# Three unread loads from GpSimd beside SyncE's stream, in a fused attention and gated-MLP decode kernel

## The chip, the core and the metric

The kernel runs on one core of one Trainium2 chip. The metric is the device time of one execution in microseconds. Before the change it is 127.67 us, the median of three runs (127.45 to 127.72).

## What is computed

One token of width 576 is normalised, and three terms are added: the token itself, an attention over the last 4,096 positions of a cache with 16 key/value heads (32 query heads), and a gated MLP.

```python
xn = _layernorm(x)
q = (xn @ wq)                               # 32 heads of 128
k, v = last W = 4096 rows of the caches     # 16 heads, each used by two query heads
p = softmax(q k^T * Dh ** -0.5)
A = (p v) @ wo
z = gelu(xn @ w_in)                         # 4608 wide
z1, z2 = z[:2304], layernorm(z[2304:])
B = (z1 * (w_sp * z2 + b_sp)) @ w_out
out = x + A + B
```

All inputs are bfloat16. The caches' last 4,096 positions are 16.8 MB each, the four weights together 17.4 MB, so some 51 MB pass from HBM into the core's buffers for one row of output.

## The kernel before

**Loads.** Nearly all bytes are loaded by SyncE, with each load covering all 128 partitions, in an order written out by hand (L104 to L119): wq in two pieces, then the caches in four batches of four heads each, mixed as k0, k1, v0, k2, v1, k3, then win, v2, v3, wo in two pieces and wout in four. One batch of k or v is 4 MB, 32 KB for each partition. ScalarE issues five tiny loads (x_row in three pieces, two scalars).

**Buffers.** The loaded tiles share two pools of two buffers each under one tag "u". A tile of SMALL width has 16,384 elements a partition: k0 to k3, v2 and wout. A tile of LARGE width has 20,736: wq, v0, v1, win, v3 and wo, in this order, so that wq, v1 and v3 use one buffer in turn and v0, win and wo the other. A batch of k or v fills only the first 16,384 elements (NU * DH). In v0, v1 and v3 the last 4,352 elements of each partition stay unused. A load into a buffer waits until the readers of the tile before it are done, and it waits for the writes of the tile before it.

**Work.** `turn(b)` transposes a batch of keys on VectorE (L209, eight pieces). `scores(b)` multiplies them with the query on TensorE (L254), takes the maximum and the exponential. `values(b)` multiplies the probabilities with a batch of v (L288) and reads only the first NU * DH elements of a tile. `z_all` and `gate` do the MLP's first half from win (L311). The order is turn and scores of batch 0 and 1, values 0, turn and scores 2, values 1, turn and scores 3, z_all and gate, values 2 and 3.

**End.** `row_of` (L376) adds up the output row in two banks: x_row, 32 row blocks of wo, 18 row blocks of wout. VectorE and ScalarE copy the two halves out (L388, L389), and SyncE and ScalarE store them.

**GpSimd** makes constants at the start: an identity, two cleared tiles (xw, zq) and two copies of the identity (L145, L147). The page counts 3.9 us of work for it, and its last instruction, the copy to perm, starts at 4.14 us. It issues no loads.

The scheduler is set to manual: each engine runs its instructions in the order of the program, and the waits between engines follow from the tiles that are read and written.

Of the kernel before, what the change touches and what calls it, by code (L numbers as in the profile page):

```python
# [18 lines left out]
DH = 128  # L19
# [6 lines left out]
NU = W // NJ  # L26
# [16 lines left out]
def kernel(  # L43
# [14 lines left out]
    nc = tc.nc  # L58
# [42 lines left out]
    kn, vn = {}, {}  # L101
# [43 lines left out]
    nc.gpsimd.tensor_copy(rep4[:], ident[:].rearrange("p (g q) -> p g q", g=4).unsqueeze(2).to_broadcast([P, 4, 4, 32]))  # L145
    perm = const.tile([P, 32, 4], BF16, name="perm")
    nc.gpsimd.tensor_copy(perm[:], ident[:].rearrange("p (q h) -> p h q", q=4))  # L147


    twice = const.tile([64, P], BF16, name="twice")  # L150
# [270 lines left out]
```

## Time and profile before

| | |
|---|---|
| median of three runs | 127.67 us |
| profiled execution | 127.53 us |
| its span | 125.7 us |
| mean granted TensorE clock | 0.81 |
| TensorE busy | 78.6 us (62% of the span) |
| VectorE busy | 64.3 us (51%) |
| ScalarE busy | 10.2 us (8%) |
| GpSimd busy | 3.9 us (3%) |
| data moved | 51.03 MB in 2,467 packets, mean 406 GB/s |

The page gives the busy time of each engine, the DMA queues with their packets, bytes and share of the time of all 16 DMA engines, the chain of work that ended last, and the groups of instructions with what they waited for. Busy shares are means over the whole span, and the stages differ, so stretches of the span are asked for one by one. "SPq" is SyncE's issuing of loads, which is not counted as busy time. Queue q1 carries SyncE's transfers, q10 those of ScalarE, q8 and q14 instructions.

### The profile page before, as it was taken

To read this page: it belongs to the slowest core of one execution; us is meant where nothing else is said; L and a number is where in the kernel's file an instruction comes from. 1 tells how busy PE (TensorE), PEld (TensorE's weight loads), DVE (VectorE), ACT (ScalarE), POOL (GpSimd) and SP (SyncE) were. 2 spreads that over 40 slices of the span, in tenths; PEclk is the share of its full clock that TensorE was granted. 3 is DMA by queue.
4 is the path that set the end of the run, shared out by engine and by line. 5 is a ranking of instruction groups with operands and counts; after the bars stand their busy time and mean duration, and the time that the engine had idled before them with its cause. 6 is when DMAs were issued, how large, how long until landed. Compare 5 with 4: busy or idle time off the path is not lost.

```text
span 125.7 us, 1318 instructions
## 1 busy us (share of the span) xinstructions
PE 78.6 (62%) x534; PEld 37.6 (30%) x534; DVE 64.3 (51%) x129; ACT 10.2 (8%) x19; POOL 3.9 (3%) x10
## 2 busy tenths in 40 slices
PE   0042750099823998297599646699375097969861
PEld 0032220034211333145234223234063044435540
DVE  6315233499839995330999451999444830010001
ACT  2101000000030000301000031000120011010001
POOL 8400000000000000000000000000000000000000
PEclk9999998559996589755559999689976855595899
DMA  4999899998999989899898999999899999999950
GB/s 102 515 420 438 382 480 438 396 490 365 480 427 394 480 365 490 386 448 469 375 480 386 497 422 422 414 397 480 386 459 443 386 432 442 393 430 411 411 207 0
DMA packets 2467, 51.03 MB, mean 406 GB/s; under 512 B 284, under 2 KB 414, under 8 KB 670
## 3 DMA queue, kind: packets, MB, share of 16 engines
q1 hardware_dynamic: 2450, 50.96, 95.0%
q8 instruction: 4, 0.07, 0.2%
q14 instruction: 1, 0.01, 0.0%
q10 hardware_dynamic: 12, 0.00, 0.0%
HBM read 50.96 MB, written 0.00 MB: 405 GB/s over the span
## 4 chain that ended last, share of the span: by engine, by line
PE 43%; DMA 37%; DVE 10%; ACT 5%; SPq 2%; issue 1%; ACTq 0%
PE s L254 30%; DMA wout<-in_B_w_out_dram 19%; DMA k<-in_A_k_cache_dram 18%; PE pv L288 4%; ACT p L274 4%; DVE kt L209 4%; PE z L311 3%; PE op L296 2%; DVE sm L257 2%; PE tr L265 2%; SPq L92 2%; PE fin L376 1%; PE su L278 1%; DVE pt L276 1%; DVE m L267 1%
## 5 line engine op out<-in xcount | busy, mean ns | idle before, releaser
L254 PE MATMUL s<-kt,zq 128*128 128x512 bf16 x128 | 37.2, 456 | 11.1 <-DVE kt L209 11.1
L209 DVE STREAM_TRANSPOSE kt<-k 128x1024 f32<-128x1024 f32 x32 | 36.4, 1205 | 3.9 <-DMA k<-in_A_k_cache_dram 3.9
L254 PEld LDWEIGHTS <-zq 128*128 128x128 bf16 x128 | 14.4, 112 | 32.8 <-issue 22.1
L288 PE MATMUL pv<-v,pt 128*32 128x512 bf16 x128 | 12.4, 557 | 0.0
L274 ACT ACTIVATE p<-sm,nm 128x1024 bf16<-128x1024 f32 x4 | 4.6, 1147 | 67.9 <-DVE nm L270 67.9
L299 DVE TENSOR_TENSOR o_t<-op,rm 128x8 bf16<-128x8 f32 x4 | 0.7, 166 | 17.2 <-PE op L296 17.2
L276 DVE STREAM_TRANSPOSE pt<-p 128x1024 bf16<-128x1024 bf16 x4 | 5.0, 1245 | 5.4 <-ACT p L274 5.4
L296 PE MATMUL op<-selu,pvs 128*128 128x8 f32 x32 | 5.9, 311 | 2.9 <-ACT pvs L293 2.9
L257 DVE CUSTOM_DVE_ANT_1 sm<-s,cm 128x512 f32<-128x512 f32 x8 | 5.4, 671 | 3.7 <-PE s L254 3.7
L296 PEld LDWEIGHTS op<-selu,pvs 128*128 128x128 f32 x32 | 5.5, 259 | 5.8 <-ACT pvs L293 5.8
L278 PE MATMUL su<-sel,l 128*128 128x8 f32 x8 | 1.8, 293 | 7.6 <-ACT p L274 7.6
L218 PE MATMUL q_ps<-wq,xw 128*32 128x512 bf16 x36 | 4.2, 626 | 3.0 <-DVE xw L187 2.4
L376 PE MATMUL fin<-wo,o_p 128*1 128x288 bf16 x64 | 5.8, 357 | 0.1
L156 PE MATMUL x_ps<-one_bf,x_row 1*64 1x1 bf16 x9 | 1.2, 248 | 7.4 <-DMA x_row<-in_A_x_dram 7.4
L288 PEld LDWEIGHTS <-pt 128*32 128x32 bf16 x128 | 4.0, 128 | 5.6 <-issue 4.8
L388 DVE CAST res<-fin 1x288 bf16<-1x288 f32 x1 | 0.4, 446 | 9.9 <-PE fin L376 9.9
L265 PE MATMUL tr<-ident_f,m 128*128 128x128 f32 x8 | 1.9, 326 | 3.9 <-DVE m L263 3.9
L376 PEld LDWEIGHTS <-o_p 128*1 128x1 bf16 x64 | 3.4, 103 | 2.3 <-DVE o_p L370 0.3
L278 PEld LDWEIGHTS su<-sel,l 128*128 128x128 f32 x8 | 1.4, 218 | 8.4 <-ACT p L274 8.4
L311 PE MATMUL z<-win,xw 128*32 128x288 bf16 x72 | 3.8, 392 | 0.0
L376 PE MATMUL fin<-wout,hv 128*1 128x288 bf16 x36 | 2.6, 285 | 1.5 <-DMA wout<-in_B_w_out_dram 1.5
L293 ACT COPY pvs<-pv 128x512 f32<-128x512 f32 x4 | 2.3, 585 | 14.3 <-PE pv L288 14.3
(88 smaller groups left out, 39.0 us busy)
## 6 DMA issues: line engine op xcount, KB each, us to landing
k<-in_A_k_cache_dram SPq DMA_DIRECT2D x4, 4096.0 KB
v<-in_A_v_cache_dram SPq DMA_DIRECT2D x4, 4096.0 KB, 39.0
win<-in_B_w_in_dram SPq DMA_DIRECT2D x1, 5184.0 KB
wq<-in_A_wq_dram SPq DMA_DIRECT2D x1, 3584.0 KB
wo<-in_A_wo_dram SPq DMA_DIRECT2D x1, 2880.0 KB
wo<-in_A_wo_dram SPq DMA_DIRECT2D x1, 1728.0 KB, 20.0
wout<-in_B_w_out_dram SPq DMA_DIRECT2D x1, 1296.0 KB
wq<-in_A_wq_dram SPq DMA_DIRECT2D x1, 1024.0 KB, 4.9
```

Of the source, the lines that this page charges most:

```text
L209: nc.vector.transpose(t[:].rearrange("p c n e -> p (c n e)").bitcast(FP32), kn[b][:, UK * DH * k:UK * DH * (k + 1)].bitcast(FP32).rearrang ...
L218: nc.tensor.matmul(q_ps[32 * g:32 * g + 32, :], lhsT=xw[:, r, :], rhs=wq_t[:, 2048 * r + 512 * g:2048 * r + 512 * (g + 1)], start=r == 0, ...
L254: nc.tensor.matmul(s_ps[:], lhsT=zq[:, b, ce, ZPAD - 8 * k4:ZPAD - 8 * k4 + P], rhs=kt[b, 4 * kk + k4][:, c, :, e], start=k4 == 0 and ce = ...
L257: nc.vector.tensor_tensor_reduce(out=sm[:, kk, :].rearrange("p (n s) -> p n s", s=HB), in0=s_ps[:].rearrange("p (n s) -> p n s", s=HB), in ...
L265: nc.tensor.matmul(tr[:], lhsT=m1[:].to_broadcast([P, P]), rhs=ident_f[:], start=True, stop=True)
L274: nc.scalar.activation(p[:], sm[:].rearrange("p k n -> p (k n)"), ACT.Exp, bias=nm[:], accum_out=l[:])
L276: nc.vector.transpose(p_t[b][:].rearrange("p k u m -> p (k u m)"), p[:])
L278: nc.tensor.matmul(su[:], lhsT=l[:].to_broadcast([P, P]), rhs=sel8[:], start=True, stop=True)
L288: nc.tensor.matmul(pv[32 * g:32 * g + 32, :].rearrange("p (n d) -> p n d", n=4), lhsT=p_t[b][:, kk, u, :], rhs=v4[:, kk, u, :, :], start=k ...
L296: nc.tensor.matmul(op[:], lhsT=pvs[:, DH * u:DH * (u + 1)], rhs=selu[:, 8 * u:8 * u + 8], start=u == 0, stop=u == 3)
L311: nc.tensor.matmul(zp[i][32 * g:32 * g + 32, :], lhsT=xw[:, r, :], rhs=win_t[:, FH * r + a:FH * r + a + HW], start=r == 0, stop=r == NR - ...
L376: nc.tensor.matmul(fin[g][32 * g:32 * g + 1, :], lhsT=col, rhs=w[:, HW * g:HW * (g + 1)], start=start, stop=stop, tile_position=(0, 32 * g))
```

## The change

Behind the copy to perm, GpSimd issues three loads. Each one takes eight rows (partitions 64, 68, ... 92) and, for each row, two parts from w_out that lie 1,024 rows of it apart. The parts have 32, 2,112 and 1,984 elements: 64, 4,224 and 3,968 bytes. The first and the second load go into the unused end of v0, the third into that of v1. Nothing reads what they bring.

```diff
     perm = const.tile([P, 32, 4], BF16, name="perm")
     nc.gpsimd.tensor_copy(perm[:], ident[:].rearrange("p (q h) -> p h q", q=4))
+
+
+    few = B_w_out[0:2048, :].rearrange("(m i r) n -> i m (r n)", m=2, i=8)
+    for b, a, n in ((0, 0, 32), (0, 64, 2112), (1, 0, 1984)):
+        nc.gpsimd.dma_start(
+            vn[b][64:96:4, NU * DH + a:NU * DH + a + 2 * n].rearrange("i (m c) -> i m c", m=2), few[:, :, a:a + n])
```

In the program that is built, TensorE, VectorE and ScalarE have the same instructions in the same order as before. GpSimd has three DMA issues more. The first waits for the same semaphore count that v0's cache load reaches on completion, the third for that of v1's. On SyncE, the load of win waits for the first two new loads in addition, and the load of v3 for the third.

## The prediction

> **What bounds the kernel now.** I first read the page's slices and DMA queues, because the change adds nothing but transfers.
>
> ```profile
> DMA  4999899998999989899898999999899999999950
> ...
> q1 hardware_dynamic: 2450, 50.96, 95.0%
> q8 instruction: 4, 0.07, 0.2%
> ...
> q10 hardware_dynamic: 12, 0.00, 0.0%
> ```
>
> The DMA row is 8 or 9 tenths in every slice from the second to the 38th. Queue q1 holds SyncE's loads: 50.96 MB in 95.0% of 16 engines' span, which is 0.95 x 16 x 125.7 = 1,910.6 engine-us, so one DMA engine moves 26.7 B/ns and sixteen 427 GB/s. The busy time by stretches (columns: length, PE, PEld, DVE, ACT and POOL busy, granted clock, DMA share, GB/s) shows where the stream starts and stops:
>
> ```profile
> 4.00:120.00 116.00, 76.23 (x504) 36.30 (x506) 60.89 (x124) 8.53 (x17) 0.53 (x2) 0.79 1.00 430
> 118.00:120.00 2.00, 1.36 (x24) 0.84 (x22) 0.00 (x0) 0.00 (x0) 0.00 (x0) 1.00 0.99 396
> 120.00:122.00 2.00, 1.16 (x21) 0.72 (x18) 0.00 (x0) 0.00 (x0) 0.00 (x0) 1.00 0.56 212
> 122.00:124.00 2.00, 1.17 (x18) 0.62 (x14) 0.45 (x1) 0.39 (x1) 0.00 (x0) 1.00 0.04 15
> ```
>
> From 4 to 120 us the engines are at share 1.00, with no gap to fill. At the end they do not stop together: 0.56, then 0.04. The last bytes come from a few engines that run late.
>
> Next I asked whether SyncE ever issues too late, since its loads wait for free buffers. Its timeline:
>
> ```profile
> 33.66 0.54 SPq L98 DMA_DIRECT2D v<-in_A_v_cache_dram  x1
> 47.78 0.54 SPq L98 DMA_DIRECT2D k<-in_A_k_cache_dram  x1
> 57.38 0.34 SPq L92 DMA_DIRECT2D win<-in_B_w_in_dram  x1
> 69.17 7.79 SPq L98 DMA_DIRECT2D v<-in_A_v_cache_dram  x2
> 96.15 0.81 SPq L92 DMA_DIRECT2D wo<-in_A_wo_dram  x2
> ```
>
> When wo is issued at 96.15 us, everything except wo (4.72 MB) and wout (2.65 MB) has been issued: 43.59 MB. Up to 96.1 us the profile counts 423 GB/s, so 40.65 MB have moved, and 2.9 MB, or 6.9 us of stream, are still queued. The same sum gives 16 us of queue when v3 is issued (76.4 us) and 14 us at win (57.38 us). So the queue never runs dry. The long PE and DVE rows of the chain of waits (L254, L209) are how a buffer comes free, and they have at least 6.9 us of slack. The end of that chain is the part that holds:
>
> ```profile
> 97.48 24.29 DMA wout<-in_B_w_out_dram
> 121.78 0.04 issue
> 121.82 1.39 PE fin L376 x18
> 123.21 0.43 DVE res L388
> ```
>
> The last 18 matmuls start as a piece of wout lands. The kernel ends when the slowest DMA engine has emptied its queue, plus a fixed tail of about 4 us.
>
> **The change, part by part.** It removes nothing. PE, DVE and ACT keep their instructions and their order; GpSimd gets three DMA issues after perm (L147), its last work, and SyncE gets two more semaphores to wait for.
>
> *When the loads run.* The first writes tile v0 and so waits, in the built program, for the completion of v0's cache load, which was issued ahead of it; the third waits the same way for v1's. The page gives 39.0 us to landing for v, and v0 was issued at 5.63: 44.6 us. v1 comes 8.39 MB later, at 430 GB/s 19.5 us: 64.1 us. Nothing stands behind these waits on GpSimd, so the waits cost nothing.
>
> *The new waits on SyncE.* win must wait for the first two loads, v3 for the third. win is issued at 57.38, 12.8 us after 44.6; v3 at 76.4, 12.3 us after 64.1. The nearest row for a load behind a full queue is a piece of wo at 20.0 us to landing, but that is time in its own queue. These loads come on a queue of their own, like q10's. Five small loads of q10 stand in the packet records one after another between 4.7 and 11.2 us, about 1.07 us each, that is behind one 28 KB packet of q1 each time. At a turn of 1.2 us per 32 KB packet, two or three turns are under 4 us. Taken at nothing. If the cover of 12 us were gone, win would still have 14 us and v3 16 us of queue ahead of them. What would be late next is the issue of wo, with 6.9 us. [...]
>
> *The bytes.* 16 x (64 + 4,224 + 3,968) = 132,096 B. Nothing hides them, since the engines have no idle time between 4 and 120 us: every byte pushes back what is queued behind it. Evenly over 16 engines it is 8,256 B each, at 26.7 B/ns 0.31 us.
>
> *The packets.* The packet records show 9 ns for a completion mark and 20 to 22 ns for a packet of 384 B. Four to six such small pieces per engine make about 0.05 us.
>
> *Bounds of the sum.* Below: zero, if only engines that do not end last get the bytes. Above: the slower foreign packets of the trace are q8's. Four packets of 16 KB took 0.2% of 16 x 125.7 = 4.0 us, 1.0 us each, or 16 B/ns. By that, 8,256 B take 0.50 us. If the same eight engines got all three loads, it would be 16,512 B, 0.62 us at q1's rate and 1.0 us at q8's. I take q1's rate, evenly, because these loads go from the same memory into the same buffers as q1's, while q8 carries instructions: 0.31 + 0.05 = 0.36 us.
>
> [...]
>
> *The sum.* The profiled execution took 127.53 us, 1.8 us more than its span of 125.7, and lies 0.14 under the median of 127.67. 127.53 + 0.36 = 127.89; on the median, 128.03 us. The three runs spread over 0.27 us, so 0.2% (0.26 us) is about what a measurement of this kernel can tell from no change. The forecast is just past it.
>
> **The rivals.**
>
> *The late engines are spared (not slower).* The end is set by few engines, as the 0.56 and 0.04 show; most stop earlier. If all three loads fall on the same eight engines and the late ones are among the other eight, the extra 0.67 us passes in their slack, and the time stays 127.67 (at a share of 0.56, 0.44 x 2 us = 0.9 us of the mean engine is idle between 120 and 122 us). It decides as soon as no late engine gets a row. For it: few late engines. Against: it needs both one fixed set of eight and the late ones outside it. Chance 0.12.
>
> *All on the late ones.* The same fixed set, with a late engine in it: 0.62 + 0.05, 128.34 us. [...] Chance 0.10.
>
> *A foreign packet is dear.* Changing queues costs as q8's packets do, 0.50 us plus 0.05, or more where the packet of q1 behind it restarts slowly: up to 0.8 us, 128.2 to 128.5 us. For it: q8's 16 B/ns. Against: q10's small loads ran beside the stream with the share at 1.00. Chance 0.13.
>
> *Each load has a fixed price on the stream.* The first piece of wq, 1 MB, landed after 4.9 us, and its bytes are 2.5 us at 427 GB/s, so 2.4 us were not bytes. Three times that is 7.3 us: 135 us. Against: it is latency of an empty queue. The five small loads of q10 fell into full stretches and left no hole. The same holds for a fixed price at launch, of which the profile has no row: with 0.5 to 1.5 us the time would be 128.5 to 129.5. Chance 0.04 together. [...]
>
> *Faster.* The late engines are late for something other than their own bytes, and q8's four packets of 1.0 us are the candidates. If the shifted stream made these fetches fall on engines when they have time to spare, up to that 0.9 us could come back at the end, 126.8 us. Nothing in the change moves PE's instructions, so I see no reason for it. Chance 0.11.
>
> **How the numbers follow.** The forecast, 0.36 us evenly on all engines, has 0.50; its own range with the spread of the runs is 127.85 to 128.25. Predicted: 128.03 us. For 8 in 10 the range leaves out the far part of the faster case and the fixed prices and takes in the spared and the dear ones: 127.55 to 128.5. Slower by over 0.2% (above 127.93) is most of the forecast (0.41 of its 0.50), the two dearer cases and the fixed price, 0.27: 0.68. Within 0.2% are the spared case's 0.12 and 0.08 of the forecast: 0.20. Faster is the last case's 0.11 and 0.01 of the forecast: 0.12.
>
> **What would show it.** Right: a third kind of packets, 48 of data and 0.13 MB, on a new queue at about 45 and 65 us; the share still 1.00 from 4 to 120; SyncE's issue of win, v3 and wo within 0.2 us of before; and the last wait of PE on wout ending about 0.36 us later than 121.78, with the same tail. Wrong: win or v3 issued later, a hole in the DMA share near 45 or 65 us, a last landing that has not moved, or a longer stretch around an unchanged span.

## The result and the profile after

The changed kernel takes 128.37 us, the median of four runs (128.29 to 128.49), against 127.65 us for the kernel before in four runs of the same measurement. The medians differ by 0.72 us. The ratio is 1.0062, with a 95% interval of 1.0050 to 1.0075, which makes 0.79 us, at least 0.6 and at most 1.0. The forecast was 128.03, so the direction and the wide range (127.55 to 128.5) held, but the measured loss is twice the forecast one and lies outside the forecast's own range of 127.85 to 128.25.

The profiled execution took 128.39 us with a span of 126.6 us. The 1.8 us around the span are as before, so the loss is inside. First the page's DMA queues (packets, MB, share of 16 engines):

```profile
q1 hardware_dynamic: 2450, 50.96, 94.6%
q0 software_dynamic: 112, 0.13, 0.3%
q8 instruction: 4, 0.07, 0.2%
```

The three loads are there on a queue of their own, q0. The line of q1 holds the surprise. The same 2,450 packets and the same bytes now take 0.946 x 16 x 126.6 = 1,916 engine-us, 5 more than the 1,911 of before (one digit of the share is worth 2). The packet records of the trace, added up, say 1,910.9 before and 1,915.4 after. SyncE's own packets have become slower, beyond being pushed back by the new ones.

The timelines of GpSimd and SyncE, from the loads on:

```profile
44.74 1.25 POOL L152 DMA_DIRECT2D v<-in_B_w_out_dram  x2 [40.20 <-DMA v<-in_A_v_cache_dram]
64.85 0.56 POOL L152 DMA_DIRECT2D v<-in_B_w_out_dram  x1 [18.86 <-issue]
```

```profile
57.27 0.33 SPq L92 DMA_DIRECT2D win<-in_B_w_in_dram  x1
69.06 7.80 SPq L98 DMA_DIRECT2D v<-in_A_v_cache_dram  x2
96.07 0.81 SPq L92 DMA_DIRECT2D wo<-in_A_wo_dram  x2
```

The loads are issued when the caches' batches v0 and v1 have landed (their last marks, in the table below, are at 44.02 and 63.80 us). win, v3 and wo are issued within 0.2 us of before, so the new waits delay nothing. The end, as stretches (the last two columns are DMA share and GB/s) and as the end of the chain:

```profile
4.00:120.00 116.00, 75.94 (x498) 36.16 (x499) 60.91 (x124) 8.53 (x17) 2.34 (x5) 0.79 1.00 429
118.00:120.00 2.00, 0.98 (x16) 0.57 (x13) 0.00 (x0) 0.00 (x0) 0.00 (x0) 1.00 0.99 399
120.00:122.00 2.00, 1.27 (x18) 0.78 (x18) 0.00 (x0) 0.00 (x0) 0.00 (x0) 1.00 0.79 306
122.00:124.00 2.00, 1.36 (x18) 0.78 (x17) 0.00 (x0) 0.00 (x0) 0.00 (x0) 1.00 0.14 50
```

```profile
97.40 25.16 DMA wout<-in_B_w_out_dram
122.61 1.41 PE fin L382 x18
124.01 0.43 DVE res L394
```

The share is 1.00 throughout as before, and the piece of wout that the last 18 matmuls wait for lands at 122.56 us in place of 121.78. Behind it the tail is the same. All of the loss is in the stream.

Where in the stream? In the packet records each of SyncE's 17 loads leaves sixteen completion marks (4-byte packets; with one for the store of the output, 273 on q1). I read them as one from each of the 16 DMA engines. The earliest, middle and last of the 16 marks, in us:

| mark | before | after |
|---|---|---|
| v0 | 42.28 / 42.56 / 44.22 | 42.25 / 42.52 / 44.02 |
| k2 | 52.01 / 52.28 / 53.93 | 51.99 / 52.36 / 54.09 |
| v1 | 61.73 / 61.99 / 63.65 | 61.72 / 62.13 / 63.80 |
| k3 | 71.44 / 71.70 / 73.36 | 72.16 / 72.43 / 74.03 |
| v3 | 103.15 / 103.47 / 105.06 | 103.87 / 104.17 / 105.80 |

The second load (packets at 51 to 53 us) delays some engines and not the earliest. Behind the third (packets at 68.8 to 70.6 us) all sixteen marks are 0.62 to 0.76 us late, the earliest too, though the load has eight packets of data and so at most eight engines carry its data. Part of that is bytes: in experiment 1 below, where hardly a packet becomes slow, the earliest mark of k3 is still at 71.90 us. In the packet records of before, the 32 KB packets that start between 68 and 72 us all took their usual 1.22 us. Here 31 of them between 68.3 and 71.2 us took 0.04 to 0.38 us longer. Around the second load none of them took over 1.25 us. The third load does something to SyncE's packets that the second, of nearly the same size, does not.

### The profile page after: what moved, and what is told of

Same layout as the page of the kernel before. It is cut to its first block, busy times and chain, and to the rows that moved or that the text cites. A ratio compares the mean times of both kernels' runs of the same rounds, so it can differ in the third digit from the quotient of the medians.

```text
span 126.6 us, 1325 instructions
## 1 busy us (share of the span) xinstructions
PE 78.6 (62%) x534; PEld 37.7 (30%) x534; DVE 64.3 (51%) x129; ACT 10.2 (8%) x19; POOL 5.7 (5%) x13
## 3 DMA queue, kind: packets, MB, share of 16 engines
q1 hardware_dynamic: 2450, 50.96, 94.6%
## 4 chain that ended last, share of the span: by engine, by line
PE 43%; DMA 37%; DVE 10%; ACT 5%; SPq 2%; issue 1%; ACTq 0%
PE s L260 29%; DMA wout<-in_B_w_out_dram 20%; DMA k<-in_A_k_cache_dram 17%; PE pv L294 4%; ACT p L280 4%; DVE kt L215 4%; PE z L317 3%; PE op L302 2%; DVE sm L263 2%; PE tr L271 2%; SPq L92 2%; PE fin L382 1%; PE su L284 1%; DVE pt L282 1%; DVE m L273 1%
## 5 line engine op out<-in xcount | busy, mean ns | idle before, releaser
L394 DVE CAST res<-fin 1x288 bf16<-1x288 f32 x1 | 0.4, 446 | 10.8 <-PE fin L382 10.8
L152 POOL DMA_DIRECT2D v<-in_B_w_out_dram x3 | 1.8, 603 | 59.1 <-DMA v<-in_A_v_cache_dram 40.2
```

## The experiments

**Theory A** blames the rows. In the records a cache load of 128 rows is 128 packets of 32 KB at 1.22 us each, and the marks of successive ones are 9.7 us apart, which is eight packets to an engine. The theory supposes that the loads of eight rows run on one half of the engines and on the other in turn, and that the third one's half is not the one that brings rows 64 to 92 in the loads of 128 rows. **Theory B** is the rival from the prediction: a GpSimd load is dear by itself, for its kind or its packets. Each experiment was timed against the kernel before on the same chip, and its excess is the ratio times that kernel's median. Where a few runs pull this number, the difference of the medians stands beside it. The code cuts show new lines against the changed kernel; lines that stay, and from experiment 2 on those that are replaced, are left out. The packet records do not name the DMA engine, so none of them shows which engines carry a load or bring a row. The runs show which rows are cheap for which load.

**1. The third load to rows 0 to 28.**

```diff
-    for b, a, n in ((0, 0, 32), (0, 64, 2112), (1, 0, 1984)):
+    for b, a, n, p in ((0, 0, 32, 64), (0, 64, 2112, 64), (1, 0, 1984, 0)):
         nc.gpsimd.dma_start(
-            vn[b][64:96:4, NU * DH + a:NU * DH + a + 2 * n].rearrange("i (m c) -> i m c", m=2), few[:, :, a:a + n])
+            vn[b][p:p + 32:4, NU * DH + a:NU * DH + a + 2 * n].rearrange("i (m c) -> i m c", m=2), few[:, :, a:a + n])
```

> Edit: the third load goes to rows 0, 4, ... 28 of v1's unused end, no longer to rows 64 to 92. Measured so far: the changed kernel is 0.72 us slower, of which the bytes explain 0.36; from the first landing of k3 (72.65 against 71.90 us) on, all sixteen DMA engines are 0.75 us late, also those that do not carry the third load. Theory A (rows): the three loads take the DMA engines in two halves in turn, and the third one runs on the half that does not serve rows 64 to 92 in the 128-row loads; its bytes are paid twice, by the engines that carry them and by those that serve the rows. With rows 0 to 28 they are paid once: +0.36 us over the kernel before, near 128.0, and GB/s in the stretch 68 to 72 us no longer falls. Theory B (the third load is dear by itself, for its 7,936-byte packets or for its moment): the rows do not matter, +0.72 us, near 128.4.

Measured: 128.10 us, ratio 1.0033 (1.0021 to 1.0045), +0.42 us. Nothing differs but the partitions that the third load writes. The page's line of q1, with a span of 126.4 us, is back at 1,911 engine-us, and near the third load two 32 KB packets take over 1.25 us, against some thirty in the change:

```profile
q1 hardware_dynamic: 2450, 50.96, 94.5%
q0 software_dynamic: 112, 0.13, 0.3%
```

The expected sign in GB/s was a poor choice. The stretch 68 to 72 us reads 506 before, 368 after and 424 here, but the engines run nearly in step with 32 KB packets (before, fourteen of the sixteen marks of k3 lie within 0.55 us), and a short stretch catches a packet more or less: before, the stretches of 2 us between 4 and 118 us read 307 to 601 GB/s. The marks and the packets' time are the measure. The third load is not dear by itself, and B falls.

**2. The second load to rows 0 to 28.**

```diff
+    for b, a, n, p in ((0, 0, 32, 64), (0, 64, 2112, 0), (1, 0, 1984, 64)):
```

The rest is as in experiment 1.

> Edit: the second load goes to rows 0, 4, ... 28 of v0's unused end; the third stays at rows 64 to 92. Theory A: now both large loads run on the half that does not serve their rows, and both are paid twice: +0.72 and another 0.3, about +1.0 us, near 128.7, with a second fall of GB/s near 52 us. Theory B: the second load is as cheap as in the changed kernel: +0.72 us, near 128.4.

Measured: 128.93 us, ratio 1.0107 (1.0085 to 1.0128), +1.37 us, which one run of 129.84 pulls up (by the medians +1.22). The same second load, cheap in the changed kernel, is now dear: the earliest mark of v1 is at 62.02 us and the middle one at 62.63 (61.72 and 62.13 in the changed kernel). In the packet records q1's packets take 1,925.5 engine-us, 14.6 more than before, and 32 KB packets of over 1.25 us stand around both loads, 20 at the second and 24 at the third. The loss is somewhat larger than A's 1.0.

**3. Without the third load.**

```diff
+    for b, a, n in ((0, 0, 32), (0, 64, 2112)):
```

> Edit: the third load is left out; the first and the second stay. Both theories: the second load delays only the eight engines that carry it, by 8,448 B at 26.7 B/ns = 0.32 us. If an engine that ends last is among them, +0.35 us, near 128.0; if all of them are in the other half, no change, near 127.65. It prices the second load alone, and by the difference to the changed kernel the third.

Measured: 128.01 us, ratio 1.0019 (1.0003 to 1.0034), +0.24 us. The earliest mark of k3 stays at 71.48 us (71.44 before), so not every engine is late, and still the end moves, if only just clear of noise. That fits a late engine among those that carry the bytes: the last mark of k3 goes from 73.36 to 73.99 us.

**4. Without the first load.**

```diff
+    for b, a, n in ((0, 64, 2112), (1, 0, 1984)):
```

> Edit: the first load (64-byte parts) is left out. If the loads take the two halves of the DMA engines in turn, the second load now runs on the half that the third had. Theory A: the second load is then the one on the half that does not serve its rows and is paid twice, the third once: again about +0.7 us, near 128.35, but the loss is seen near 52 us (the landing of k2 and v1 late on all engines) and not near 70 us. Theory B: the third load stays dear near 70 us, +0.7 us. If there is no turn (the same eight engines for each load), leaving out 1 KB changes nothing, neither the time nor the place.

Measured: 128.59 us, ratio 1.0063 (1.0050 to 1.0076), +0.80 us. The place was not where I expected it, for a reason of its own: without the small load ahead of it the 4,224-byte load waits for nothing and is issued at 4.48 us. (In the change the small load is the first on its queue too, and it does wait for v0. Why the two differ is not shown.) Its packets lie between 8.2 and 10.8 us, and all engines are late from there on (the second piece of wq has its earliest mark at 13.81 us against 13.22). The 32 KB packets between 68 and 72 us are of their usual length. That fits A, but place and turn changed together, so it was done again.

**5. The first load twice.**

```diff
+    for b, a, n in ((0, 0, 32), (0, 0, 32), (0, 64, 2112), (1, 0, 1984)):
```

> Edit: the first load (64-byte parts) is issued twice, the second copy behind the first one's completion; the other two loads as in the changed kernel. It asks whether the loads take the two halves of the DMA engines in turn. If they do, one small load more swaps the halves: the second load is now the one on the half that does not serve rows 64 to 92, and the third is on the half that does. Theory A with turns: the time stays near that of the changed kernel (+0.7 us, 128.4), but the loss on all engines moves from 70 to the completion of the second load, near 55 us, so that SyncE's data already move slower in the stretch 52 to 60 us and the stretch 68 to 72 us is whole. Without turns: the fall of GB/s stays at 68 to 72 us.

Measured: 128.51 us, ratio 1.0063 (1.0051 to 1.0075), +0.80 us. A load of 1 KB more swaps the parts of the two large ones. The slow packets stand between 58.6 and 61.5 us, at the second load (issued from 52.58 us on, with a copy of the first in front). v1's earliest mark is at 62.28 us in place of 61.72, and around the third load no packet is slow. This is what A's turns by halves of the engines would do, and one fixed set of eight would not.

**6. The same bytes over all rows.**

```diff
+    nc.gpsimd.dma_start(vn[1][:, NU * DH:NU * DH + 516], B_w_out.rearrange("(p r) n -> p (r n)", r=FR)[:, 0:516])
```

> Edit: in place of the three loads, one load from GpSimd brings the same 132,096 B in 128 rows of 1,032 B into v1's unused end. Theory A: no engine writes rows of another one, the bytes are paid once and evenly: 132,096 B at 427 GB/s = 0.31 us, and with the packets 0.35 us, near 128.05. Theory B (a load from GpSimd in the full stream is dear whatever its rows): +0.7 us.

Measured: 128.11 us, ratio 1.0031 (1.0019 to 1.0044), +0.40 us (by the medians +0.49). This is the plain price of 132 KB, near what experiment 1 gave. Here the packets run between 21.8 and 23.9 us, and no 32 KB packet around them is slow.

**7 and 8. The second load alone, issued by ScalarE, to high and to low rows.**

```diff
+    nc.scalar.dma_start(
+        vn[0][64:96:4, NU * DH + 64:NU * DH + 64 + 2 * 2112].rearrange("i (m c) -> i m c", m=2), few[:, :, 64:64 + 2112])
```

> Edit: GpSimd issues nothing; ScalarE issues the second load alone, to rows 64 to 92 of v0's unused end, behind its five small loads and at the start of the kernel. Theory A holds for any issuer: if its eight rows go over the eight engines that serve rows 0 to 63, all sixteen engines are late, +0.6 to +0.7 us, near 128.35; if over the others, +0.3 or nothing. Theory C (only loads from GpSimd collide): +0.3 or nothing.

> Edit: as the run before, but to rows 0 to 28. Theory A: the opposite of the run to rows 64 to 92: if that one is at +0.6 to +0.7 us, this one is paid once, +0.3 us or nothing (nothing if none of the engines that end last carries it); the two differ by 0.3 us or more. Theory C: the two are the same.

Measured: to rows 64 to 92, 128.34 us, ratio 1.0056 (1.0044 to 1.0068), +0.71 us; to rows 0 to 28 (`0:32:4`), 128.00 us, ratio 1.0039 (1.0016 to 1.0063), +0.50 us. The second interval is wide because three of its twelve runs are near 129.0, of which more below; the other nine lie between 127.75 and 128.13, and by the medians the two are +0.72 and +0.38 us. The two intervals overlap, so the times alone do not decide. The packets do: q1's take 1,920.4 engine-us with the high rows and 1,910.5, as before, with the low ones. The collision, as I call it when a load makes SyncE's packets slow, does not need GpSimd.

**9 and 10. Four neighbouring rows, and four rows four apart.** If only those engines pay that carry the bytes or bring the rows in the loads of 128, it should matter how many engines bring the four rows. How many do is not shown; four rows are four of a cache load's 128 packets, so four engines at most.

```diff
+    for b, a, n in ((0, 0, 2112), (1, 0, 2112)):
+        nc.gpsimd.dma_start(
+            vn[b][64:68, NU * DH + a:NU * DH + a + 2 * n].rearrange("i (m c) -> i m c", m=2), few[0:4, :, a:a + n])
```

> Edit: in place of the three loads, two loads of four rows each, two parts of 4,224 B to a row, into rows 64 to 67 of v0's and v1's unused ends: 67,584 B in all, half of the change's bytes. [...] Without A (bytes count only on the engines that carry them): 8,448 B or 16,896 B to an engine, at most +0.65 us.

> Edit: the same two loads into rows 64, 68, 72 and 76. [...] Without A: the same time as the run before.

Measured: rows 64 to 67, 128.94 us, ratio 1.0112 (1.0070 to 1.0153), +1.43 us (by the medians +1.18, since one run took 130.01); rows 64, 68, 72 and 76 (`64:80:4`), 128.87 us, ratio 1.0091 (1.0074 to 1.0107), +1.16 us. In both, and in the next two, the loads run early: their packets lie near 8 to 11 us and 22 to 25 us. The two can't be told apart, and both cost more than the +0.65 us that bytes alone would cost at most. In the second of them all sixteen marks of k0 are late: the earliest is at 23.51 us in place of 22.90, and so behind the last one of before, at 23.46. (In experiment 11, of the same bytes without a collision, the earliest is at 23.16.) With rows 64 to 67 the last mark of k0 is 1.4 us behind the middle one (25.59 against 24.18 us; before, 23.46 against 23.18). A's bookkeeping, "paid twice, by those who carry and those who serve", is wrong. A collision holds up all engines.

**11 and 12. Four rows again, in two orders.**

```diff
+    for b, p, n in ((0, 0, 2112), (1, 16, 2112)):
+        nc.gpsimd.dma_start(
+            vn[b][p:p + 16:4, NU * DH:NU * DH + 2 * n].rearrange("i (m c) -> i m c", m=2), few[0:4, :, 0:n])
```

The second of the two has 16 and 0 exchanged.

> Edit: the two four-row loads of the last two runs, the first into rows 0, 4, 8 and 12, the second into rows 16, 20, 24 and 28. The last two runs were +1.2 and +1.1 us and did not differ, and all sixteen engines were late in both, so a collision is not paid by the engines alone that carry the rows or serve them. If the turns go by four here, the first load runs on the first four engines and the second on the next four, each on engines that serve these rows. Theory A1 (an engine that writes rows served by another one holds up all): no collision, 16 KB of bytes on eight engines each 8,448 B, +0.3 us or nothing, near 127.95. Theory A2 (only writing from the lower half's engines into rows of the upper half holds up all): the same. Theory A3 (loads of four rows are dear by themselves): +1.1 us.

> Edit: as the run before, with the two sets of rows exchanged, so that each load writes rows that other engines of the same half serve. Theory A1: both loads collide, +0.8 to +1.1 us, near 128.7. Theory A2: no load leaves its half, the same time as the run before, +0.3 us or nothing. Theory A3: +1.1 us in both.

Measured: 128.00 us, ratio 1.0030 (1.0019 to 1.0041), +0.38 us, with the first order; 128.86 us, ratio 1.0093 (1.0077 to 1.0109), +1.19 us, with the sets exchanged. The pages' lines of q1, first of the cheap kernel (span 126.1 us), then of the dear one (span 127.3 us):

```profile
q1 hardware_dynamic: 2450, 50.96, 94.8%
```

```profile
q1 hardware_dynamic: 2450, 50.96, 94.7%
```

That is 0.948 x 16 x 126.1 = 1,913 engine-us and 0.947 x 16 x 127.3 = 1,929. The bytes, the loads and the eight rows are the same; only which load gets which four rows differs. In the packet records no 32 KB packet around the second load of the cheap kernel is over 1.25 us, and some sixty are in the dear one. Both times are near what A1 forecast (+0.3 or nothing, and +0.8 to +1.1), by which it counts whether the engine that carries a row is the one that brings this row in the 128-row loads. That stays a reading, since no record names an engine.

What the runs show is the pattern. Rows 64 to 92 were cheap for the second load in the change and dear for the third (no slow packet and 31), and rows 0 to 28 were dear for the second in experiment 2 and cheap for the third in experiment 1 (20 slow packets and two). One more small load in front moved the slow packets from the third load to the second (experiment 5). For ScalarE's load, rows 64 to 92 were dear and rows 0 to 28 cheap (experiments 7 and 8), and in 11 and 12 the order of the same eight rows made the price. That all engines are held up is read from all sixteen marks being late, of k3 in the change and of k0 in experiment 10.

## Why the prediction was half right

**What bounds the kernel** was right: an unbroken stream, whose end moves the kernel's end by as much. The landing before the last 18 matmuls moved 0.78 us, the profiled time 0.86 us.

**When the loads run and the new waits** were right within their covers. Issue was computed for 44.6 and 64.1 us and came at 44.74 and 64.85. The time to land was not under 4 us but 6.9, 9.1 and 7.8 (last column); the 12 us of cover held it:

```profile
v<-in_B_w_out_dram POOLq DMA_DIRECT2D x1, 66.0 KB, 9.1
v<-in_B_w_out_dram POOLq DMA_DIRECT2D x1, 62.0 KB, 7.8
v<-in_B_w_out_dram POOLq DMA_DIRECT2D x1, 1.0 KB, 6.9
```

Part of the miss was to be seen before: in q10's records a load's data packet and its mark can stand a turn apart (5.82 and 6.90 us), so a load can pay more than one turn. And about 4 us pass between issue and the first packet, which starts at 48.7 us for the first load and at 68.8 for the third. The reason given for the first wait, that the load writes tile v0, is not enough either: in experiments 4 and 9 to 12 the first load into v0 is issued at 4.5 us.

SyncE's waits have new entries for the loads, ahead of win (L92) and of v3 (L98). Both are issued at their old times all the same, because PE's values are done later, by 2.6 and 3.6 us:

```profile
SPq L92 <- DMA v<-in_B_w_out_dram: 6.3, 1, 6.3
SPq L92 <- PE pv L294: 2.6, 1, 2.6
SPq L98 <- DMA v<-in_B_w_out_dram: 3.0, 1, 3.0
SPq L98 <- PE pv L294: 3.6, 1, 3.6
```

**The bytes and packets, 0.36 us**, were right as the price of these bytes where nothing collides: 0.42, 0.40 and 0.38 us in experiments 1, 6 and 11. (The last has half the bytes; on how many engines they lie is not shown.) The count of packets was off: 32 of data, not 48. The two parts of 64 or of 3,968 bytes for a row stand in the records as one packet of 128 or 7,936, those of 4,224 as two.

**The step that failed** is the choice among the bounds of the sum: q1's rate "because these loads go from the same memory into the same buffers as q1's". It is the term for the third load that was mis-sized. I counted bytes on engines, and did not ask whether it matters which rows they go to. By the medians, of 0.72 us 0.39 are bytes and 0.33 the third load's rows (experiment 1 against the change).

**The rivals.** The dear foreign packet (128.2 to 128.5 us) has the measured number but not the cause: loads from GpSimd in the full stream cost their bytes alone in experiments 1, 6 and 11, and one from ScalarE is dear in experiment 7. So it is luck that the wide range, which reached to 128.5 for this rival, took in the result. All on the late ones (128.34) has the number too, but one fixed set of eight is out by experiment 5. That late engines are spared did not come about: the change, and each load that was tried, moved the end (the least by 0.24 us, experiment 3); which engines are the late ones, no record names. A fixed price for each load is out, since three loads cost 0.42 us in experiment 1 and one load of the same bytes 0.40 in experiment 6; no run shows one at launch of 0.5 to 1.5 us. Nothing came back for the faster case.

**Open.** Why a load to such rows holds up all sixteen engines was not settled, nor what sets the price. By the medians, experiments 1, 8 and 11, without a collision, are at +0.39, +0.38 and +0.37 us. With one colliding load the change is at +0.72, experiments 4 and 5 at +0.88 and +0.89 and 7 at +0.72; with two, experiments 2, 9, 10 and 12 are at +1.22, +1.18, +1.11 and +1.23. So each colliding load adds 0.33 to 0.5 us. In 9, 10 and 12 a load has half the rows and about half the bytes of the others, so the price does not follow them. No version beat the kernel before, which has none of this work.

## What to carry to other kernels

Where a kernel is one unbroken DMA stream, a transfer is not small because its bytes are few: here 0.13 MB beside 51 cost 0.72 us. Time a load of few rows with other rows, and with all 128. By the medians, the three loads cost 0.72 or 0.39 us by the rows of the third alone (the change and experiment 1), ScalarE's load 0.72 or 0.38 (7 and 8), and the same bytes over all rows 0.49 (6). In the profile, multiply the main queue's share by the span: if the same packets take more engine time than before, as here 1,916 engine-us in place of 1,911, something holds them up. Short stretches of GB/s did not show it here. Price such an edit with a twin that moves the same bytes without the suspected trait, as experiments 1, 6 and 11 do here.

## What was not expected of the hardware

The tail was longer where the granted clock in it was lower. In the profiled execution of experiment 8 the last 18 matmuls ran at a granted clock of 0.50 from 122 us on and took 2.37 us, not 1.41 as in the changed kernel at a clock of 1.00, though the wout piece had landed 0.5 us sooner than in the changed kernel:

```profile
95.46 26.58 DMA wout<-in_B_w_out_dram
122.08 2.37 PE fin L381 x18
124.44 0.43 DVE res L393
```

This 1.0 us is what sets this run, of 128.87 us, apart from the nine near 127.95. The two others near 129.0 have no profile, but nearly the same mean granted clock (0.859 to 0.860 in all three, at most 0.824 in the nine). Of the single runs of 129.84 and 130.01 us in experiments 2 and 9, the profile of the first shows 2.36 us for the same 18 matmuls, with the clock at 0.50 from 124 us on, and that of the second a chain that ends in PE work. The kernel before has two single runs of 128.52 and 128.60 us, without a profile.
